# The first 512 tokens of a two-layer SiLU block: five transposes of one contraction tile in place of three, in another order among the weight slabs, and ScalarE's warm-up ahead of the start barrier

## The chip, the core and the metric

The kernel runs on one core of one Trainium2 chip. The metric is the device time of one execution in microseconds (us). Before the change the median of three runs is 124.7 us (124.01 to 125.0). A profile of one further execution gives the time of each instruction and each transfer.

## The reference

Two matrix products with a SiLU between them; inputs and outputs are bfloat16.

```python
B, S, D, F = 1, 2048, 640, 1728
x:  (1, 2048, 640)     w1: (640, 1728)     w2: (1728, 640)

h = jnp.einsum("bsd,df->bsf", x, w1)
h = silu(h)
out = jnp.einsum("bsf,fd->bsd", h, w2)
```

## The kernel before, in words

**Tiles.** The contraction of the first product, D = 640, is cut into five tiles of 128 (`DT`, index k). F = 1728 is cut into 13 tiles of 128 (`FT`, index ft) and a rest of 64. The 2048 tokens are cut into four parts of 512 (`SCH`, index c). The first product needs x with the contraction on the partitions, so every piece of x is brought in by a DMA that transposes it: `turned(c0, c1, k0, k1)` (line 90) brings contraction tiles k0 to k1 of tokens c0 to c1 into `xT`. `w1` comes in slabs: `slab(eng, k, f0, f1)` (line 118) brings tiles f0 to f1 of contraction tile k into `w1s`. Each transfer has a semaphore of its own, and TensorE waits on it where the tile is first read.

**Order of the first product, tokens 0 to 511.** The core has eight accumulation banks (`NO` = 8). For these tokens the loop is turned around: for k = 0 to 4, TensorE sweeps over ft = 0 to 7, one bank each (`sweep`, line 188), so that a sweep needs one slab and one tile of x and not all five. A step is a pair of matmuls, one for each half of 64 output partitions, running beside each other. Sweeps 0 to 2 are in `opening` (line 193); sweep 3 and sweep 4 follow, and after each bank of sweep 4 ScalarE applies SiLU into `hT` (line 175). Slab 0 is cut in two: tiles 0 to 4 (`NA` = 5) come by ScalarE's queue, tiles 5 to 7 by SyncE's (`ld_w1b`), awaited ahead of bank 5. Then come ft = 8 to 12 for the same tokens, from two more loads (`ld_rest`, `ld_rest2`); then tokens 512 on, which wait for all five of their transposes (`ld_xc[c]`, line 159); then the rest of 64, and the second product, whose results are copied out by VectorE and ScalarE and stored.

**What is issued early.** At its start every engine goes through a barrier: it reports that it has arrived and waits for the others. `early(emit, engine, arrived)` (line 98) moves the instructions that `emit` makes ahead of that point of `engine`: with `arrived=False` ahead of the engine's report, so that the barrier opens only after them; with `arrived=True` (only `opening` on TensorE) behind its report, ahead of its wait. All loads for k = 0 to 4 are early on SyncE, one slab is early on ScalarE, and the clearing of `z` is early on VectorE. SyncE issues in the order in which the code stands, and everything after the barrier on this queue (the two rest loads, 15 transposes for the later tokens, `w2`) comes behind the early part.

**The clock and the tables.** Until the first operands have landed, TensorE multiplies zeros (`first_dummies`, line 135): 13 matmuls of 256 columns and one pair of half width. ScalarE applies SiLU to a small cleared tile `warm` (line 153), before which its table load stands; `warm` is cleared by GpSimd at line 140. Both stand behind the barrier.

Of the kernel before, what the change touches and what calls it, by code (L numbers as in the profile page):

```python
# [5 lines left out]
ACT = mybir.ActivationFunctionType  # L6
# [3 lines left out]
def bass_standalone__dense_activation_silu__prompt_kernel(  # L10
# [13 lines left out]
    P = 128  # L24
    NB = 8
    BANK = 512
    DT = D // P
    FT = F // P
    FL = F - FT * P
    SCH = 512  # L30
# [8 lines left out]
    pe, act, dve, pool, sp = nc.tensor, nc.scalar, nc.vector, nc.gpsimd, nc.sync  # L39

    with ExitStack() as es:
        def sb(name, shape, dtype):
            return es.enter_context(nc.sbuf_tensor(name, shape, dtype))
# [9 lines left out]
        warm = sb("warm", [P, 32], fp32)  # L53
# [6 lines left out]
        def sem(name):  # L60
            s = es.enter_context(nc.semaphore(name))
            count[s.name if hasattr(s, "name") else name] = 0
            return [s, 0]

        def tick(ins, s, n=1):
            ins.then_inc(s[0], n)
            s[1] += n
            return (s, s[1])

        def wait(eng, *points):  # L70
            for pt in points:
                if pt is None:
                    continue
                s, v = pt
                key = (id(eng), id(s))
                if seen.get(key, 0) < v:
                    eng.wait_ge(s[0], v)
                    seen[key] = v

        s_pe, s_act, s_dve = sem("s_pe"), sem("s_act"), sem("s_dve")  # L80
        s_pool = sem("s_pool")
# [3 lines left out]
        def load(eng, out_ap, in_ap):  # L85
            s = sem(f"s_ld{n_dma[0]}")
            n_dma[0] += 1
            return tick(eng.dma_start(out=out_ap, in_=in_ap), s, 16)

        def turned(c0, c1, k0, k1):  # L90
            s = sem(f"s_tr{n_dma[0]}")
            n_dma[0] += 1
            return tick(sp.dma_start_transpose(
                out=xT[:, k0:k1, c0:c1], in_=xf[c0:c1, k0 * P:k1 * P]), s, 16)

        ET = mybir.EngineType

        def early(emit, engine, arrived=True):
            n = len(nc.main_func.blocks[0].instructions)
            r = emit()  # L100
            lst = nc.main_func.blocks[0].instructions
            new = lst[n:]
            del lst[n:]
            at = next(
                i for i, ins in enumerate(lst)
                if ins.opcode == ("EventSemaphore" if arrived else "Drain") and ins.engine == engine
            )
            lst[at:at] = new
            return r
# [8 lines left out]
        def slab(eng, k, f0=0, f1=NO):  # L118
            return load(eng, w1s[:, k, f0 * P:f1 * P], w1_v[:, k, f0 * P:f1 * P])

        ld_w1 = {}
        ld_t = {}
        ld_t[0] = ld_t[1] = early(lambda: turned(0, SCH, 0, 2), ET.SP, False)
        ld_w1[0] = early(lambda: slab(act, 0, 0, NA), ET.Activation, False)
        p_z = early(lambda: tick(dve.memset(z[:, :], 0.0), s_dve), ET.DVE, False)  # L125

# [2 lines left out]
        def dummies(n, w):  # L129
            for _ in range(n):  # L130
                for c0 in range(0, P, w):
                    pe.matmul(ps[c0:c0 + w, 3, 0:HB], lhsT=z[:, 0:w], rhs=z[:, :],  # L132
                              start=True, stop=True)

        def first_dummies():
            wait(pe, p_z)
            dummies(13, P)
            dummies(1, HC)

        p_warm = tick(pool.memset(warm[:, :], 0.0), s_pool)  # L140

        ld_w1b = early(lambda: slab(sp, 0, NA, NO), ET.SP, False)
        ld_w1[1] = early(lambda: slab(sp, 1), ET.SP, False)
        ld_w1[2] = early(lambda: slab(sp, 2), ET.SP, False)
        ld_t[2] = early(lambda: turned(0, SCH, 2, 3), ET.SP, False)
        ld_w1[3] = early(lambda: slab(sp, 3), ET.SP, False)
        ld_t[3] = ld_t[4] = early(lambda: turned(0, SCH, 3, DT), ET.SP, False)
        ld_w1[4] = early(lambda: slab(sp, 4), ET.SP, False)
        CM = CO + 2 * P
        ld_rest = load(sp, w1s[:, :, CO:CM], w1_v[:, :, CO:CM])  # L150
        ld_rest2 = load(sp, w1s[:, :, CM:F], w1_v[:, :, CM:F])
        wait(act, p_warm)
        act.activation(out=warm[:, :], in_=warm[:, :], func=ACT.Silu)  # L153

        ld_xc = {}
        for c in range(1, NSC):
            s = sem(f"s_xc{c}")
            for dt in range(DT):
                ld_xc[c] = tick(sp.dma_start_transpose(
                    out=xT[:, dt, c * SCH:(c + 1) * SCH],  # L160
                    in_=xf[c * SCH:(c + 1) * SCH, dt * P:(dt + 1) * P],
# [31 lines left out]
        def opening():  # L193
            first_dummies()
            wait(pe, ld_t[0], ld_w1[0])
            for ft in range(NO):
                if ft == NA:
                    wait(pe, ld_w1b)
                part(0, ft, 0, SCH, start=True)
            for k in (1, 2):  # L200
                sweep(k, 0, SCH, ld_w1[k], ld_t[k])
# [208 lines left out]
```

## Time and profile before

| | before |
|---|---|
| median of three runs | 124.7 us (124.01 to 125.0) |
| profiled execution | 124.91 us |
| its span, first to last instruction | 123.4 us |
| TensorE busy | 121.1 us, 98% of the span |
| ScalarE busy | 38.8 us |
| VectorE busy | 7.0 us |
| HBM read, written | 4.51 MB, 2.62 MB |

The issues on SyncE's queue up to the transposes of tokens 512 to 1023, with the time from the issue's start to the landing:

| what | issued at, us | to landing, us |
|---|---|---|
| x, k = 0 and 1 | 0.00 | 3.7 |
| w1, k = 0, ft 5 to 7 (96 KB) | 1.38 | 3.8 |
| w1, k = 1 (256 KB) | 2.00 | 3.8 |
| w1, k = 2 | 2.53 | 4.0 |
| x, k = 2 | 3.01 | 4.1 |
| w1, k = 3 | 4.20 | 3.7 |
| x, k = 3 and 4 | 4.82 | 4.1 |
| w1, k = 4 | 6.10 | 4.4 |
| w1, ft 8 and 9, all k (320 KB) | 7.09 | 4.3 |
| w1, the rest, all k (560 KB) | 7.53 | 5.5 |
| x, tokens 512 to 1023, five transposes | from 8.10 | the fifth 3.3 |

On ScalarE's queue the first 160 KB of slab 0 are issued at 0.12 and land after 2.7 us.

In the profile, PE is TensorE, PEld its weight loads, ACT ScalarE, DVE VectorE, POOL GpSimd and SP SyncE; a q behind an engine's name marks its issuing part. "L171" is line 171 of the kernel. A row of the timeline has the start, the duration, the engine, line and operation, and, in brackets, how long the engine was idle before and what ended that. The chain of waits is followed back from the last instruction: at each step to whatever released it.

### The profile page before, as it was taken

The numbers are of one execution on the slowest core, as the hardware profiler recorded it, in microseconds if no ns is written. First come the engines' busy times: TensorE is split into PE (matmuls) and PEld (weight loads), VectorE is DVE, ScalarE is ACT, GpSimd is POOL, SyncE is SP. The second block draws the span as 40 slices with busy tenths as digits, with TensorE's granted clock in tenths as the row PEclk, the third lists the DMA queues.
The fourth block names the chain that finished last, engine by engine and source line by source line (L and its number), as shares of the span: only waits on it lengthen the run. The fifth ranks groups of instructions, "written<-read, shape, count | busy, mean of one in ns | idle before, by whom it ended". The sixth has DMA issues, their size and how long they took to land.

```text
span 123.4 us, 2299 instructions
## 1 busy us (share of the span) xinstructions
PE 121.1 (98%) x1057; PEld 59.5 (48%) x1057; DVE 7.0 (6%) x11; ACT 38.8 (31%) x67; POOL 0.3 (0%) x5
## 2 busy tenths in 40 slices
PE   8999999999999999999999999999999999999993
PEld 5455555555555555555544444444444444444452
DVE  0000000000000000000000022002201300222001
ACT  0041985555555555555530011001101200110110
POOL 0000000000000000000000000000000000000000
PEclk9999999999999999999999999999999999999999
DMA  6999945475992000000000005202200220022112
GB/s 142 234 271 302 157 103 108 94 75 92 288 391 70 0 0 0 8 0 0 0 0 5 0 5 115 56 0 106 106 0 5 106 106 0 5 106 106 53 74 86
DMA packets 19482, 10.42 MB, mean 84 GB/s; under 512 B 13457, under 2 KB 18961, under 8 KB 19473
## 3 DMA queue, kind: packets, MB, share of 16 engines
q1 hardware_dynamic: 19184, 10.05, 32.1%
q10 hardware_dynamic: 288, 0.23, 0.8%
q8 instruction: 8, 0.13, 0.5%
q14 instruction: 2, 0.01, 0.0%
HBM read 4.51 MB, written 2.62 MB: 58 GB/s over the span
## 4 chain that ended last, share of the span: by engine, by line
PE 95%; DMA 3%; ACT 0%; issue 0%
PE ps L171 95%; DMA xT<-in_x_dram 3%; ACT o_sb L254 0%
## 5 line engine op out<-in xcount | busy, mean ns | idle before, releaser
L171 PE MATMUL ps<-xT,w1s 128*64 128x512 bf16 x540 | 59.2, 382 | 0.1
L171 PE MATMUL ps<-w2s,hT 64*128 64x512 bf16 (+3 forms) x377 | 46.2, 369 | 0.0
L171 PEld LDWEIGHTS ps<-xT,w1s 128*64 128x64 bf16 x540 | 30.5, 111 | 28.6 <-issue 0.9
L175 ACT ACTIVATE hT<-ps 128x512 bf16<-128x512 f32 x52 | 30.0, 607 | 22.9 <-PE ps L171 22.9
L171 PEld LDWEIGHTS ps<-w2s,hT 64*128 64x128 bf16 (+1 forms) x377 | 21.0, 95 | 24.1 <-issue 0.2
L254 ACT CAST o_sb<-ps 128x512 bf16<-128x512 f32 (+1 forms) x9 | 5.0, 551 | 41.5 <-PE ps L171 41.5
L171 PE MATMUL ps<-hT,w2s 64*128 64x512 bf16 x104 | 11.7, 376 | 0.0
L171 PEld LDWEIGHTS ps<-hT,w2s 64*128 64x128 bf16 x104 | 5.0, 94 | 6.3 <-issue 0.4
L252 DVE CAST o_sb<-ps 128x512 bf16<-128x512 f32 (+1 forms) x8 | 5.4, 675 | 40.5 <-PE ps L171 40.5
L252 DVE CAST oT<-ps 128x512 bf16<-128x512 f32 x2 | 1.4, 692 | 73.8 <-PE ps L171 73.8
L254 ACT CAST oT<-ps 128x512 bf16<-128x512 f32 x2 | 1.2, 586 | 10.6 <-PE ps L171 10.6
L132 PE MATMUL ps<-z 128*128 128x256 bf16 (+1 forms) x15 | 3.3, 419 | 0.4 <-DVE z L125 0.4
L153 ACT ACT_TABLE_LOAD x1 | 1.3, 1283 | 7.1 <-DVEq L395 7.1
L171 PE MATMUL ps<-w2t,hTt 64*128 64x512 bf16 (+2 forms) x17 | 2.9, 363 | 0.0
L132 PEld LDWEIGHTS ps<-z 128*128 128x128 bf16 (+1 forms) x15 | 1.9, 142 | 1.5 <-issue 0.4
L175 ACT ACTIVATE hTt<-ps 128x512 bf16<-128x512 f32 x2 | 1.2, 597 | 1.0 <-PE ps L171 1.0
L171 PEld LDWEIGHTS ps<-w2t,hTt 64*128 64x128 bf16 x17 | 0.9, 94 | 1.1
L171 PE MATMUL ps<-hTt,w2t 64*128 64x512 bf16 x4 | 0.8, 376 | 0.0
L171 PEld LDWEIGHTS ps<-hTt,w2t 64*128 64x128 bf16 x4 | 0.2, 94 | 0.2
L153 ACT ACTIVATE warm<-warm 128x32 f32<-128x32 f32 x1 | 0.2, 229 | 0.0
L125 DVE MEMSET z<- 128x128 uint32 x1 | 0.2, 165 | 0.2 <-issue 0.2
L140 POOL MEMSET warm<- 128x32 f32 x1 | 0.1, 125 | 6.7 <-POOLq L395 6.7
(4 smaller groups left out, 0.4 us busy)
## 6 DMA issues: line engine op xcount, KB each, us to landing
out_dram<-o_sb SPq DMA_DIRECT2D x15, 160.0 KB, 1.8
w2s<-in_w_dram SPq DMA_DIRECT2D x1, 1120.0 KB, 6.1
w1s<-in_w_dram SPq DMA_DIRECT2D x4, 256.0 KB, 3.9
w2s<-in_w_dram SPq DMA_DIRECT2D x1, 960.0 KB, 8.4
w1s<-in_w_dram SPq DMA_DIRECT2D x1, 560.0 KB, 5.5
w1s<-in_w_dram SPq DMA_DIRECT2D x1, 320.0 KB, 4.3
xT<-in_x_dram SPq DMA_TRANSPOSE x18, 3.9
w1s<-in_w_dram ACTq DMA_DIRECT2D x1, 160.0 KB, 2.7
```

The costliest lines, as they stand in the source:

```text
L125: p_z = early(lambda: tick(dve.memset(z[:, :], 0.0), s_dve), ET.DVE, False)
L132: pe.matmul(ps[c0:c0 + w, 3, 0:HB], lhsT=z[:, 0:w], rhs=z[:, :], start=True, stop=True)
L140: p_warm = tick(pool.memset(warm[:, :], 0.0), s_pool)
L153: act.activation(out=warm[:, :], in_=warm[:, :], func=ACT.Silu)
L171: return pe.matmul(o, lhsT=l, rhs=r, start=start, stop=stop, skip_group_check=shared)
L175: r = tick(act.activation(out=out_ap, in_=in_ap, func=ACT.Silu), s_act)
L252: r = tick(dve.tensor_copy(out=out_ap, in_=in_ap), s_dve)
L254: r = tick(act.copy(out=out_ap, in_=in_ap), s_act)
```

## The change

The first 512 tokens' five contraction tiles are brought in by five transposes of one tile each instead of three (tiles 0 and 1, tile 2, tiles 3 and 4). The order on SyncE's queue becomes: x tile 0; rest of slab 0; slab 1; x tiles 1 and 2; slab 2; slab 3; x tiles 3 and 4; slab 4. TensorE multiplies zeros ten times instead of thirteen ahead of the half-width pair. The clearing of `warm` and ScalarE's SiLU on it move ahead of these engines' reports at the barrier. What each sweep waits for is the same by name: slab k and x tile k.

```diff
-        ld_t[0] = ld_t[1] = early(lambda: turned(0, SCH, 0, 2), ET.SP, False)
+        ld_t[0] = early(lambda: turned(0, SCH, 0, 1), ET.SP, False)
         ld_w1[0] = early(lambda: slab(act, 0, 0, NA), ET.Activation, False)
...
         def first_dummies():
             wait(pe, p_z)
-            dummies(13, P)
+            dummies(10, P)
             dummies(1, HC)
 
-        p_warm = tick(pool.memset(warm[:, :], 0.0), s_pool)
+        p_warm = early(lambda: tick(pool.memset(warm[:, :], 0.0), s_pool), ET.Pool, False)
+
+        def warm_up():
+            wait(act, p_warm)
+            act.activation(out=warm[:, :], in_=warm[:, :], func=ACT.Silu)
+
+        early(warm_up, ET.Activation, False)
 
         ld_w1b = early(lambda: slab(sp, 0, NA, NO), ET.SP, False)
         ld_w1[1] = early(lambda: slab(sp, 1), ET.SP, False)
+        ld_t[1] = early(lambda: turned(0, SCH, 1, 2), ET.SP, False)
+        ld_t[2] = early(lambda: turned(0, SCH, 2, 3), ET.SP, False)
         ld_w1[2] = early(lambda: slab(sp, 2), ET.SP, False)
-        ld_t[2] = early(lambda: turned(0, SCH, 2, 3), ET.SP, False)
         ld_w1[3] = early(lambda: slab(sp, 3), ET.SP, False)
-        ld_t[3] = ld_t[4] = early(lambda: turned(0, SCH, 3, DT), ET.SP, False)
+        ld_t[3] = early(lambda: turned(0, SCH, 3, 4), ET.SP, False)
+        ld_t[4] = early(lambda: turned(0, SCH, 4, 5), ET.SP, False)
         ld_w1[4] = early(lambda: slab(sp, 4), ET.SP, False)
         CM = CO + 2 * P
         ld_rest = load(sp, w1s[:, :, CO:CM], w1_v[:, :, CO:CM])
         ld_rest2 = load(sp, w1s[:, :, CM:F], w1_v[:, :, CM:F])
-        wait(act, p_warm)
-        act.activation(out=warm[:, :], in_=warm[:, :], func=ACT.Silu)
```

## The prediction

> **What bounds the kernel now.** I read the chain of waits first. In order of time it is:
>
> ```profile
> 0.00 3.72 DMA xT<-in_x_dram
> 3.72 0.04 issue
> 3.76 117.77 PE ps L171 x1041
> 121.53 0.02 issue
> 121.55 0.27 ACT o_sb L254
> ```
>
> From 3.76 us to 121.53 the chain never leaves TensorE. The total of its idle time before matmuls at line 171 is 0.1 us. So two things alone can move the end: when the real matmuls begin and at what clock, and whether one of them has to wait later on. The change touches only the loads of the first 512 tokens, so the next view is the timeline of the first 18 us (start, duration):
>
> ```profile
> 0.00 1.33 SPq L93 DMA_TRANSPOSE xT<-in_x_dram  x1
> 0.39 3.31 PE L132 MATMUL ps<-z 128*128 128x256 bf16 x15 [0.39 <-DVE z L125]
> 1.38 1.58 SPq L88 DMA_DIRECT2D w1s<-in_w_dram  x3
> 3.01 1.15 SPq L93 DMA_TRANSPOSE xT<-in_x_dram  x1
> ...
> 3.76 0.18 PEld L171 LDWEIGHTS ps<-xT,w1s 128*64 128x64 bf16 x4 [0.36 <-DMA xT<-in_x_dram]
> ...
> 4.20 0.58 SPq L88 DMA_DIRECT2D w1s<-in_w_dram  x1
> 4.82 1.24 SPq L93 DMA_TRANSPOSE xT<-in_x_dram  x1
> 5.42 11.55 PEld L171 LDWEIGHTS ps<-xT,w1s 128*64 128x64 bf16 x108 [0.19 <-issue]
> 6.10 1.95 SPq L88 DMA_DIRECT2D w1s<-in_w_dram  x3
> 8.10 9.81 SPq L159 DMA_TRANSPOSE xT<-in_x_dram  x7
> ```
>
> The reader sees SyncE issuing without a pause, and that a transpose holds it for about the same time whether it carries one contraction tile (1.15) or two (1.33, 1.24). A slab holds it for 0.43 to 0.58. TensorE's pairs of half steps start at 3.76, 4.19, 4.62 and 5.05, 0.43 apart, and from 5.42 on 0.215 apart (54 pairs in 11.55 us). The first pairs run at half rate, though the profile's clock row shows full speed throughout; pair spacing is the better witness.
>
> Sweeps over the eight banks therefore begin at 3.76, 6.28, 8.01, 9.73 and 11.46 and end at 13.19; tiles 8 to 12 end at 18.57, where tokens 512 to 1023 are needed. Against that, the issues' times to landing, asked one by one (start + time to landing): second transpose 3.0 + 4.1 = 7.1, slab 2 at 2.5 + 4.0 = 6.5, slab 3 at 4.2 + 3.7 = 7.9, third transpose 4.8 + 4.1 = 8.9, slab 4 at 6.1 + 4.4 = 10.5, the fifth transpose of the next tokens 13.7 + 3.3 = 17.0. So every operand has just 0.8 to 1.6 us to spare. That slack is the cover that the change spends.
>
> **Part by part: the start.** The first transpose now carries one tile. No row shows such a transpose alone in front of an empty queue; the nearest are these:
>
> ```profile
> L159 SPq DMA_TRANSPOSE xT<-in_x_dram x15: 1261/1262/2413, 8.1 to 28.2; - x15
> DMA to landing us min/median/max: 2.7/3.5/5.5
> ```
>
> It lands between 2.7 (the quickest one-tile transpose) and 3.7 (the double one now). I take 3.0, near the quick end, since nothing is queued before it. Ten dummies and the pair behind them end 3 x 0.215 = 0.64 us sooner, near 2.85, and the first slab from ScalarE lands at 0.12 + 2.7 = 2.8, so neither is later. Real work starts at 3.0, not 3.76. If the clock rises at the same 5.4, that adds about two pairs at half rate: six pairs to 5.5, two at 0.215, and the first sweep ends at 5.95 instead of 6.28. **Gain 0.33 us**; none if the landing stays at 3.7.
>
> [...]
>
> **The issues.** On SyncE the change replaces three transposes by five. First one 1.33 -> about 1.23 (0.09 is what one tile less is worth between 1.24 and 1.15); second 1.15, third 1.15 more, the double one 1.24 -> two of 1.15; 0.05 between issues. The new starts: transpose 0 at 0.00, rest of slab 0 at 1.28, slab 1 at 1.90, transpose 1 at 2.43, transpose 2 at 3.63, slab 2 at 4.82, slab 3 at 5.45, transpose 3 at 5.95, transpose 4 at 7.14, slab 4 at 8.33. Slab 2 moves from 2.53 by **+2.29**, slab 4 from 6.10 by **+2.23**, and with it all behind it on this queue: the two remaining slabs and fifteen transposes of the later tokens.
>
> Time to landing is the unknown. For slabs the ends are 2.7 (the 160 KB slab on ScalarE's empty queue) and 4.4 (slab 4). The nearest row is slab 3, which directly follows a one-tile transpose: 3.7. But that slab landed only 0.8 after the transpose before it, which itself had waited behind two slabs; with issues now further apart less is queued, so I take 3.4. For transposes, ends 2.7 and 4.1; I take 3.3, the row of the fifth one of line 159.
>
> - Sweep 0, bank 5: rest of slab 0 at 1.28 + 3.8 = 5.1; wanted at 3.0 + 5 x 0.43 = 5.15. No stall.
> - Sweep 1, wanted 5.95: slab 1 at 1.9 + 3.8 = 5.7, transpose 1 at 2.43 + 3.3 = 5.75 (6.5 at the far end: stall 0.6). No stall.
> - Sweep 2, wanted 7.68: transpose 2 at 6.9, slab 2 at 4.82 + 3.4 = 8.2 (7.5 to 8.8). **Stall 0.55** (0 to 1.1).
> - Sweep 3, wanted 9.93: slab 3 at 8.9, transpose 3 at 9.3 (10.05). No stall.
> - Sweep 4, wanted 11.66: transpose 4 at 10.4, slab 4 at 8.33 + 3.4 = 11.75 (11.0 to 12.7). **Stall 0.1** (0 to 1.0). The sweep ends at 13.48, 0.3 later than now.
> - The two rest slabs move to 9.32 and 9.77: 9.32 + 4.3 = 13.6 at the loaded time, wanted 13.5; 9.77 + 5.5 = 15.3, wanted 15.6. Nothing taken.
> - Tokens 512 to 1023, wanted 13.48 + 5.38 = 18.86: the fifth transpose is issued at 13.66 + 2.23 = 15.89 and lands at 19.2 (18.6 at 2.7; 20.0 at 4.1). **Stall 0.3** (0 to 1.1).
>
> In that reckoning the early gain and the first stalls don't decide: the shifted queue does. Tokens 1024 to 1535 landed about 9 us before they are wanted (20.6 + 2.8 against 18.57 + 65 x 0.215 = 32.5), and the second weight by 39, while its first use follows the last of the first product at 62.6; 2.23 us more costs nothing there.
>
> **ScalarE's warm-up** now stands before its arrival at the start barrier. Its table load ran from 7.09 for 1.28, its first real work at 11.88; it is hidden now and hidden after. If it stayed behind the barrier, which waits for SyncE, it would run at 9.3 to 10.8, before the first activation near 12. Its slab is issued first, so the load delays nothing. The cleared tile on GpSimd comes earlier by the same move, off every path. Cost 0. PE's wait at the barrier, after sweep 2, ends near 9.3, and sweep 3 starts at 9.9: also covered, but by only 0.6.
>
> **Sum.** Tokens 512 on start at 19.2 in place of 18.57: +0.6. The profiled execution took 124.91 (span 123.4 and 1.5 around it), so 125.5; the median shown is 124.7, 0.2 under it, which gives **125.3**.
>
> **Rivals.**
> 1. *The loaded landings stay* (slower). If time to landing is what one slab costs, not a queue, slab 2 comes at 8.8 and slab 4 at 8.33 + 4.4 = 12.7; sweep 4 ends at 14.46, the next part is wanted at 19.84: +1.3, 126.0. For it: the four 256 KB slabs took 3.7 to 4.4 whatever stood before them. Against: ScalarE's slab took 2.7. It decides from a slab-2 landing of about 8.6 on. Chance 0.22.
> 2. *Issue time is no bound* (faster). The DMA view, cut into 0.05 us slices, shows the double transpose moving at 260 to 310 GB/s near 2.8 us; if slabs land by 2.7 to 3.0 and line 159's first issues shrink from 1.60 to 1.26 with a shorter queue, no stall is left and the start's 0.33 stays: 124.4. Against: SyncE has no idle time up to 29 us. Chance 0.16. [...] The trace disagrees: a 128 KB transpose at such rates moves in under 0.5 us and is issued in 1.15.
> 3. *The clock rises later.* If the first transpose lands at 3.7 and the 0.85 us gap after the dummies starts the count of 5.0 us (0.39 to 5.4) anew, half rate lasts to 8.7: 3.3 us more, worth half, +1.6, 126.3. Chance 0.05.
> 4. *The first landing doesn't come earlier*, as issue time hardly shrinks. The queue's shift still decides, so the time stays 125.3; it is part of the forecast.
>
> **How the numbers follow.** Forecast 125.3 with its own range 124.9 to 125.8, chance 0.57. The whole range takes in rival 2 and most of rival 1, and a clock that rises earlier or later: 124.3 to 126.2. A measurement of this kernel can tell about 1% (1.25 us) from no change. Slower by more: most of rival 1 and rival 3, 0.22. Faster by more: hardly any case, 0.04. Within: 0.74.
>
> **What would show it.** The first pair near 3.0; a new wait of TensorE on slab 2 near 7.7 and one on xT near 18.9; line 159 starting near 10.3; the table load near 0.6. I am wrong if TensorE has no wait after 3.0 (rival 2), if slab 2 takes 3.8 or more to land (rival 1), or if pairs stay 0.43 apart beyond 5.9 (rival 3).

## The result and the profile after

The changed kernel takes 126.34 us (median of six runs, 125.91 to 126.64) against 124.5 for the kernel before (six runs, 124.01 to 125.19): ratio 1.0143, 95% interval 1.0112 to 1.0173, so about 1.8 us slower. The forecast was 125.3 with a range up to 126.2. The profiled execution took 126.50, its span is 125.0. A ratio below can differ by up to 0.2% from the quotient of the two medians, and where the runs of a kernel scatter widely, it leaves the longest out and the range of all runs is given beside it.

The chain of waits of the changed kernel, in order of time (start, duration, what; its last pieces, with the pieces before 15.96 left out):

```profile
15.96 0.04 issue
16.00 4.08 DMA xT<-in_x_dram
20.09 0.04 issue
20.13 91.60 PE ps L177 x846
111.73 0.16 issue
```

Before, the chain entered TensorE at 3.76 and stayed there. Now it runs through SyncE's issues and enters TensorE for good at 20.13, at the first matmul of tokens 512 on, which was at 18.57 before. What released it is the fifth transpose of these tokens, issued at 16.00 and 4.08 us under way. All that follows is as long as before, so 1.56 us of this trace's loss were there by 20.13.

The timeline of the changed kernel (line 177 is what was line 171, line 165 what was line 159):

```profile
0.00 1.25 SPq L93 DMA_TRANSPOSE xT<-in_x_dram  x1
0.53 1.28 ACT L144 ACT_TABLE_LOAD   x1 [0.53 <-issue]
2.38 2.44 SPq L93 DMA_TRANSPOSE xT<-in_x_dram  x2
...
2.99 0.18 PEld L177 LDWEIGHTS ps<-xT,w1s 128*64 128x64 bf16 x4 [0.23 <-DMA xT<-in_x_dram]
...
4.22 0.76 PEld L177 LDWEIGHTS ps<-xT,w1s 128*64 128x64 bf16 x8 [0.19 <-issue]
4.87 1.05 SPq L88 DMA_DIRECT2D w1s<-in_w_dram  x2
5.97 2.42 SPq L93 DMA_TRANSPOSE xT<-in_x_dram  x2
5.97 1.47 PEld L177 LDWEIGHTS ps<-xT,w1s 128*64 128x64 bf16 x16 [0.99 <-issue]
...
7.70 1.47 PEld L177 LDWEIGHTS ps<-xT,w1s 128*64 128x64 bf16 x16 [0.26 <-DMA w1s<-in_w_dram]
8.44 1.95 SPq L88 DMA_DIRECT2D w1s<-in_w_dram  x3
9.59 1.47 PEld L177 LDWEIGHTS ps<-xT,w1s 128*64 128x64 bf16 x16 [0.42 <-issue]
10.44 7.12 SPq L165 DMA_TRANSPOSE xT<-in_x_dram  x5
11.56 3.59 PEld L177 LDWEIGHTS ps<-xT,w1s 128*64 128x64 bf16 x36 [0.51 <-DMA w1s<-in_w_dram]
```

The first real matmul starts at 2.99, and the pairs, 0.43 apart at first, are 0.215 apart from 4.22 on. This close spacing, whose beginning the prediction calls the rise of the clock, began 1.2 us sooner here than in the trace before (5.42). The granted clock reads 1.0 for both profiled executions, so that a clock is behind the spacing is not shown. Yet there is now a start of weight loads with idle time in front at every sweep: 5.97, 7.70, 9.59, 11.56. By the steps between matmuls, TensorE lost 0.7 us ahead of sweep 1 (5.08 to 6.00 in place of 0.215; tile 1 landed at 5.87), nothing ahead of sweep 2, and 0.2 us ahead of each of sweeps 3 and 4. Sweep 4 begins at 11.56, 0.1 later than before in spite of the earlier start and the earlier close spacing. SyncE issues slab 2 at 4.87, slab 4 at 8.44 and line 165's first transpose at 10.44, against 2.53, 6.10 and 8.10.

Further on, the same view for 14 to 22 us:

```profile
15.85 3.43 PE L177 MATMUL ps<-xT,w1s 128*64 128x512 bf16 x30 [0.21 <-DMA w1s<-in_w_dram]
...
20.13 2.13 PE L177 MATMUL ps<-xT,w1s 128*64 128x512 bf16 x18 [0.86 <-DMA xT<-in_x_dram]
```

Two more waits, which the kernel before doesn't have at all: ahead of tile 10, for the second rest load (the step from 15.25 to 15.85 in place of 0.215, so 0.4 us), and ahead of tokens 512 on (the step from 18.87 to 20.13, so 1.0 us). The second is the larger, and what makes the transpose so late is seen in the DMA view of the changed kernel from 15.5 to 19.5 us, in slices of 0.1 us:

```profile
GB/s 187 279 287 289 402 54 249 269 269 271 201 20 0 0 0 0 5 8 10 8 10 10 10 8 13 233 287 297 292 216 197 287 292 287 193 54 79 143 179 187
...
q8 instruction: 1, 0.02, 1.8%
```

From 16.6 to 18.0 nothing but a trickle moves. In front of it, at 15.96 in the list of packets, stands the one packet of the queue for instructions, 16 KB, 1.18 us long. Such packets come again every 10 to 15 us to the end of the run (the next at 26.42, 40.15 and 54.04). They are taken here for TensorE's program code; no view says which engine's instructions they carry, but in two experiments below, with more TensorE instructions, the first one came sooner, at 15.23 and 12.99. The trace before has the same picture two microseconds sooner (packet at 13.80, standstill until 15.75), when these transposes still had 1.6 us to spare; four of the five were through at its end, and here three. The same row of its DMA view from 13.5 to 16.5 us, in slices of 0.075 us:

```profile
GB/s 297 283 287 505 97 161 123 106 184 167 167 116 137 103 85 102 82 45 24 10 27 31 10 10 10 27 10 7 10 14 243 294 294 280 294 270 15 0 0 0
```

### The profile page after: what moved, and what is told of

The parts are those of the page before. It is cut to its first block, busy times and chain, and to the rows that moved or that the text cites. A ratio compares the mean times of both kernels' runs of the same rounds, so it can differ in the third digit from the quotient of the medians.

```text
span 125.0 us, 2296 instructions
## 1 busy us (share of the span) xinstructions
PE 120.9 (97%) x1053; PEld 59.6 (48%) x1054; DVE 6.9 (6%) x11; ACT 38.9 (31%) x67; POOL 0.3 (0%) x5
## 4 chain that ended last, share of the span: by engine, by line
PE 82%; SPq 5%; DMA 3%; issue 0%; ACT 0%
PE ps L177 82%; SPq L165 4%; DMA xT<-in_x_dram 3%; SPq L88 1%; ACT o_sb L260 0%
## 5 line engine op out<-in xcount | busy, mean ns | idle before, releaser
L177 PE MATMUL ps<-xT,w1s 128*64 128x512 bf16 x540 | 59.9, 382 | 1.6 <-DMA xT<-in_x_dram 1.4
L177 PEld LDWEIGHTS ps<-xT,w1s 128*64 128x64 bf16 x540 | 31.1, 111 | 30.2 <-issue 2.1
L132 PE MATMUL ps<-z 128*128 128x256 bf16 (+1 forms) x12 | 2.7, 416 | 0.4 <-DVE z L125 0.4
L132 PEld LDWEIGHTS ps<-z 128*128 128x128 bf16 (+1 forms) x12 | 1.4, 138 | 1.3 <-issue 0.4
```

The costliest lines, as they stand in the source:

```text
L177: return pe.matmul(o, lhsT=l, rhs=r, start=start, stop=stop, skip_group_check=shared)
```

## The experiments

Theory Q: the two added issues push everything behind them on SyncE's queue back by 2.3 us, and that uses up the slack of the later loads. Theory S: the loss lies in the five sweeps, whose operands come late one by one. Ratios are to the kernel before, from the same chip and session.

**The shift alone.** The kernel before, with small loads added behind slab 4:

```diff
         ld_w1[4] = early(lambda: slab(sp, 4), ET.SP, False)
+        junk = sb("junk", [P, 5, 16], bf16)
+        for j in range(5):
+            early(lambda j=j: load(sp, junk[:, j, :], w1_v[:, 0, j * 16:(j + 1) * 16]), ET.SP, False)
```

> The kernel before, unchanged in its transposes, order, dummies and warm-up, with five loads of 4 KB each (into a tile nobody reads) added on SyncE's queue behind slab 4, still ahead of the barrier. They hold SyncE about 5 x 0.48 = 2.4 us, as the change does, but leave the loads of the first 512 tokens alone. Theory Q (what costs is the shift of everything behind the early part of SyncE's queue): line 159's fifth issue moves from 13.7 to 16.1, it lands at 19 to 20 instead of 17, is wanted at 18.6, and the time rises by 0.5 to 1.6 us, ratio 1.004 to 1.013. Theory S (what costs is the later arrival of the single tiles and slabs within the five sweeps): no change, ratio 1.000.

Measured 125.59 against 124.8, ratio 1.0059 (1.0035 to 1.0084). The timeline of TensorE's weight loads in this kernel:

```profile
9.61 8.59 PEld L174 LDWEIGHTS ps<-xT,w1s 128*64 128x64 bf16 x82 [0.62 <-issue]
19.13 1.87 PEld L174 LDWEIGHTS ps<-xT,w1s 128*64 128x64 bf16 x20 [0.94 <-DMA xT<-in_x_dram]
```

The wait ahead of tokens 512 on appears, 0.87 - 0.215 = 0.66 us. A second one, 0.3 us ahead of sweep 3 near 9.4, belongs to none of its operands: slab 3 had landed at 7.7 and the transpose at 8.6. The start barrier, which opens only when SyncE has issued its early part (9.0) and lies ahead of sweep 3, is what is left; here and in the changed kernel sweep 3 starts 0.2 us after SyncE's first issue behind the barrier (9.64 after 9.45, 9.62 after 9.43). So the shift by itself costs about 0.6%: theory Q holds, but it is less than half of the loss.

**The other parts alone.** The kernel before with `dummies(10, P)` and the warm-up moved:

> The kernel before with only the other two parts of the change: ten dummies in place of thirteen, and the warm-up and its clearing ahead of the barrier. The three transposes and the order stay. Theories Q and S alike: within 0.3 us of before, ratio 0.998 to 1.003. Theory C (the gap of 0.85 us between the dummies' end at 2.85 and the first operands at 3.7 delays the clock): up to 1.6 us slower, ratio up to 1.013, and pairs 0.43 apart up to 8 us.

Ratio 1.0017 (0.9977 to 1.0056), but the ten runs reach from 124.33 to 126.65, while the kernel before stays within 124.33 to 125.32. The median of all is 125.55 against 124.8. The profile is of one of the longer runs (126.46), and TensorE's weight loads show what it spent:

```profile
3.72 0.18 PEld L175 LDWEIGHTS ps<-xT,w1s 128*64 128x64 bf16 x4 [0.96 <-DMA xT<-in_x_dram]
...
8.42 1.67 PEld L175 LDWEIGHTS ps<-xT,w1s 128*64 128x64 bf16 x16 [0.25 <-issue]
```

The ten dummies end at 3.06, 0.6 us before the double transpose has landed (3.68), and the pairs stay 0.43 apart until 8.4. What theory C expected happened in this run; that the shortest takes 124.33, as the kernel before does, suggests that it does not happen in every one. In the changed kernel the gap isn't there, since its first transpose lands at 2.95.

**Two loads off SyncE's queue.** In the changed kernel, `ld_rest = load(act, ...)` and `ld_rest2 = load(act, ...)`:

> The changed kernel with the two loads of tiles 8 to 13 (ld_rest, ld_rest2) issued by ScalarE behind the barrier instead of SyncE, which takes about 1.0 us off SyncE's queue ahead of line 165's transposes. Theory Q: the fifth transpose is issued at 15.0 instead of 16.0 and lands about 1 us sooner, near 19.1; time about 125.4, ratio to before 1.005 to 1.010. Theory S: no change against the changed kernel, ratio 1.014.

Ratio 1.0108 (1.0076 to 1.0141), at the edge of what theory Q expected, and its trace isn't what was expected: the fifth transpose was issued at 14.55, 1.45 sooner, and landed at 19.97, practically where it did. With the rest loads on a second queue, these took 5.1 and 6.7 us to land and the transposes beside them 6.5 (median of five), against 3.4, 5.8 and 5.5 in the changed kernel. In this trace tokens 512 on start at 20.01 without a wait of their own: the close spacing began only at 7.0, and TensorE waited 0.2 us for slab 4 and 0.5 us for the first rest load (landed at 14.54). A shorter queue was paid for by slower transfers.

**The fetch of code.** In the changed kernel, three `pe.wait_ge(p_z...)` behind each dummy:

> The changed kernel with 30 waits on an already satisfied semaphore added among TensorE's dummies: same work, more instructions. In the changed kernel's trace one 16 KB transfer on the instruction queue starts at 15.96 and takes 1.18 us, and transpose packets stand still from 16.6 to 18.0; before, it came at 13.8. Theory F (this fetch of TensorE's code, met by the later tokens' transposes, is worth about 1 us of the loss): with more instructions ahead the fetch comes earlier, the fifth transpose lands near 19.0 instead of 20.1, time 125.4, ratio 1.005 to 1.010. If the fetch is only a bystander, or does not move: ratio stays at 1.014.

Ratio 1.0103 (1.0069 to 1.0138). The waits merged into 10 instructions, the packet came at 15.23 instead of 15.96, the standstill went on to 17.1, and the fifth transpose landed at 19.78, with a wait of 1.1 us for it. Not conclusive. A stronger version writes the dummies in smaller pieces:

```diff
-            dummies(10, P)
+            for _ in range(20):
+                for c0 in (0, HC):
+                    pe.matmul(ps[c0:c0 + HC, 3, 0:P], lhsT=z[:, 0:HC], rhs=z[:, 0:P],
+                              start=True, stop=True)
```

> The changed kernel with its ten dummies of 128 x 256 columns written as twenty pairs of half width and 128 columns: about the same time on TensorE, 60 more of its instructions ahead of the real work (30 waits had merged into 10 instructions and moved the code fetch little, so that run didn't decide). Theory F (the fetch of TensorE's code freezes the transposes for about 1.4 us, and costs the changed kernel about 1.2 us because it meets the fifth transpose): the fetch comes 1 to 3 us earlier than 15.96, the fifth transpose, issued near 16.0, lands by 19.0, TensorE's wait for it falls from 1.0 us to under 0.3, and the time to 125.3, ratio 1.003 to 1.008. If the fetch is a bystander: ratio 1.012 to 1.017, as for the changed kernel.

The packet moved to 12.99, the standstill after 16.6 is gone, and the fifth transpose landed 2.9 us after its issue, at 19.37, with no wait for it. But the time didn't follow: ratio 1.0157 (1.0098 to 1.0217), which is what was expected of a bystander. The timeline of TensorE in this kernel:

```profile
12.74 3.19 PE L180 MATMUL ps<-xT,w1s 128*64 128x512 bf16 x28
16.34 6.88 PE L180 MATMUL ps<-xT,w1s 128*64 128x512 bf16 x62 [0.41 <-ACT hT L184]
```

The wait moved to the second rest load, which landed at 16.20, 6.3 us after its issue; that load, not the activation that the view names, is what tile 10 had to wait for. So moving the code packet does move the standstill (transpose packets now stand still until 16.05), but no gain in time shows. In this trace TensorE lost 0.6 us to that load and 0.6 us to slab 2 (landed at 8.35). That the packet delayed the load is not shown, and the trace is of the shortest of four runs (125.94; the others 126.64 to 126.94), so what the others spent isn't seen.

**Three transposes, cut 1/2/2.** The changed kernel with tiles 1 and 2 in one transpose and tiles 3 and 4 in one:

```diff
-        ld_t[1] = early(lambda: turned(0, SCH, 1, 2), ET.SP, False)
-        ld_t[2] = early(lambda: turned(0, SCH, 2, 3), ET.SP, False)
+        ld_t[1] = ld_t[2] = early(lambda: turned(0, SCH, 1, 3), ET.SP, False)
...
-        ld_t[3] = early(lambda: turned(0, SCH, 3, 4), ET.SP, False)
-        ld_t[4] = early(lambda: turned(0, SCH, 4, 5), ET.SP, False)
+        ld_t[3] = ld_t[4] = early(lambda: turned(0, SCH, 3, 5), ET.SP, False)
```

> The changed kernel with tiles 1 and 2 in one transpose and tiles 3 and 4 in one: three transposes as before, cut 1/2/2 and not 2/1/2, the rest of the change kept. SyncE's queue is no longer than before (line 159's transposes start near 8.1). Theory Q with F (shift, and the freeze that then meets the fifth transpose): the wait for tokens 512 on is gone; what is left is the earlier start (0.3 gained) against a wait for tile 1, issued at 2.4 and landing at 6.2: 124.3 to 124.9, ratio 0.996 to 1.002. Theory S (late operands within the sweeps): 125.5 or more, ratio 1.006 and up.

Ratio 1.0030 (1.0001 to 1.0059). With the queue no longer than before, four fifths of the loss are gone. The early start (3.18) still doesn't pay: in the profiled run the close spacing began only at 6.9, and with an early one tile 1, landing at 5.9, is what sweep 1 would wait for (that second half is argued from the landing, since no trace of this kernel has an early close spacing).

**Four transposes**, only tiles 3 and 4 together:

> The changed kernel with tiles 3 and 4 in one transpose: four transposes, SyncE's queue about 1.15 us longer than before instead of 2.3. Theory Q (the shift eats the slack of the loads behind the early part): with no shift the ratio was 1.003, with the whole shift 1.014; half a shift uses up slack more than it costs, so nearer the lower one: 1.004 to 1.008. Theory S (the five single tiles, each late by its own issue): as the changed kernel up to sweep 3, 1.008 to 1.014.

Ratio 1.0090 (1.0057 to 1.0122), between the two, a little above what theory Q expected and inside what theory S did. Three, four and five transposes give 1.003, 1.009 and 1.014: each issue of 1.2 us on SyncE's queue costs about 0.7 us, the shift and the sweeps together.

**Pricing the two late waits.** First the changed kernel without the wait for tokens 512 to 1023, whose first product then reads the first 512 tokens:

```diff
-            wait(pe, ld_xc[c])
+            if c > 1:
+                wait(pe, ld_xc[1], ld_xc[c])
+            x0 = 0 if c == 1 else c * SCH
...
-                    ins = step(b, k, ft, c * SCH, (c + 1) * SCH, start=(k == 0), stop=(k == DT - 1))
+                    ins = step(b, k, ft, x0, x0 + SCH, start=(k == 0), stop=(k == DT - 1))
```

> The changed kernel, but the first product for tokens 512 to 1023 reads the first 512 tokens again and doesn't wait for its own five transposes, which are still issued and are awaited before tokens 1024 on (so the output of these tokens is that of others). All loads as before. Theory Q: the wait of 1.0 us at 19 us in the changed kernel's trace goes and nothing takes its place: 125.3, ratio 1.005 to 1.008. Theory S: the loss lies in the sweeps, and ratio stays above 1.010.

Ratio 1.0078 (1.0052 to 1.0104). Then also without the wait ahead of tile 10 (`wf = ft if ft < NO + 2 else ft - NO` picks the slab, and the load is awaited one part later):

> As the one before, and tiles 10 to 12 of the first 512 tokens read the slabs of tiles 2 to 4 and don't wait for the second rest load either. Theory Q: the wait of 0.6 us ahead of tile 10 goes too; what is left is the waits in the sweeps (1.2 us in the changed kernel's trace, of which the earlier start and clock pay most): 124.4 to 124.9, ratio 0.998 to 1.004. Theory S: ratio 1.008 or more.

Ratio 1.0056 (1.0037 to 1.0076), a little more than expected. The timeline of its weight loads from sweep 4 on is one piece:

```profile
11.56 10.50 PEld L177 LDWEIGHTS ps<-xT,w1s 128*64 128x64 bf16 x100 [0.48 <-DMA w1s<-in_w_dram]
```

Together: 1.0143 - 1.0078 = 0.0065, or 0.8 us, is the wait for the fifth transpose; 0.0022, or 0.3 us, goes with the wait for the second rest load; 0.0056, or 0.7 us, remains (each difference has an uncertainty of 0.3 to 0.4%). The 0.3 us is the least sure. In the profiled run without the wait for tokens 512 on, TensorE waited 0.4 us ahead of tile 8, for the first rest load (landed at 13.64), and not ahead of tile 10:

```profile
13.68 8.61 PE L177 MATMUL ps<-xT,w1s 128*64 128x512 bf16 x78 [0.22 <-DMA w1s<-in_w_dram]
```

Ten of the twelve runs of the kernel with neither wait lie within 125.02 to 125.17. In that kernel's trace the close spacing began at 4.5, and sweep 4 nevertheless started at 11.56, when slab 4 had landed (11.52): the pace of the sweeps is now that of the loads. So theory S has its share; that the 0.7 us lies in the sweeps is read from this trace and has no experiment of its own.

**Thirteen dummies again** in the changed kernel:

> The changed kernel with thirteen dummies again: real work starts at about 3.5 instead of 3.0, since TensorE works through the dummies first. Theory Q: the waits behind swallow it, as they did the gain; 126.2 to 126.5, ratio 1.012 to 1.016. If the early start were worth what was forecast: 0.3 slower still, ratio 1.017.

Ratio 1.0162 (1.0128 to 1.0197). Real work started at 3.49, and the fifth transpose landed at 20.23. Within the intervals this is the changed kernel's time, and the trace shows waits of 0.6 and 1.0 us at the same two places: half a microsecond at the start is worth at most a few tenths here.

**Why the second rest load is late.** The changed kernel without the fifteen transposes of tokens 512 on; the first product of these tokens, and the rest of 64, read the first 512 tokens:

```diff
-            for dt in range(DT):
-                ld_xc[c] = tick(sp.dma_start_transpose(
-                    out=xT[:, dt, c * SCH:(c + 1) * SCH],
-                    in_=xf[c * SCH:(c + 1) * SCH, dt * P:(dt + 1) * P],
-                ), s, 16)
+            ld_xc[c] = None
...
```

> The changed kernel without the fifteen transposes of tokens 512 on; these tokens' first product reads the first 512 tokens instead. Everything ahead on SyncE's queue as in the changed kernel. Theory X (transposes right behind the second rest load in the same rings hold it up): it is issued at 9.9 and lands by 14.0, and no wait is left ahead of tile 10; ratio 1.004 to 1.007, the price of the sweeps alone. Theory L (the load is slow by itself, one DMA engine being late with it): it lands near 15.7 as before, and the wait ahead of tile 10 stays; ratio 1.007 to 1.010.

Ratio 1.0080 (1.0052 to 1.0108), and from the DMA view of its issues from 9 to 14 us:

```profile
w1s<-in_w_dram SPq DMA_DIRECT2D x1, 560.0 KB, 5.6
```

Theory L: the load is late (15.41) without any transpose behind it, with loads of the second weight there instead, though the wait ahead of tile 10 is only 0.15 us in this trace. Its last 896-byte packets thin out: 132 start from 13.5 to 14.0, then 66 and 30 in the next two half microseconds, and the last ends at 15.1. That one DMA engine is late with the load, as theory L has it, is not shown. Why the packets thin out, and why the load takes 4.9 to 6.3 us over the traces with this order of loads and 4.4 from the same issue time in the first experiment, stay open.

**Loads on two queues.** Transposes cut 1/2/2, with the rest of slab 0 and slab 1 issued by ScalarE:

> As the one before (transposes 1/2/2), with the rest of slab 0 and slab 1 issued by ScalarE, ahead of its warm-up: SyncE's queue gets about 1.1 us shorter than before the change, tile 1 and 2 are issued at 1.3. Theory Q with F: first operands at 3.0 to 3.3, no wait in the sweeps, tokens 512 on in time: 0.3 us faster than before, ratio 0.995 to 0.999. A rival R (two queues with transposes and slabs side by side slow each other, as the rest loads on ScalarE's queue did, where the first later transpose took 6.5 us to land): first operands at 3.5 or later and waits in sweeps 1 and 2, ratio 1.002 to 1.010.

Ratio 1.0146 (1.0077 to 1.0215), above what rival R expected. The first transpose landed at 3.61 and not at 3.0, as R had it, but the waits in the sweeps that R named aren't there: the dummies left a gap of 0.6 us, and the close spacing began at 7.4. With only the rest of slab 0 on ScalarE's queue:

> Transposes cut 1/2/2 as in e1_three (ratio 1.003), with only the rest of slab 0 moved to ScalarE's queue, ahead of its warm-up. SyncE's queue gets 0.6 us shorter than before the change, tiles 1 and 2 are issued at 1.8 and land by 5.3. Theory Q (only a longer queue costs): the early start pays at last, ratio 0.996 to 1.000. Rival R (loads from two queues in flight together delay the first transpose, as in e8_two_queues, where it landed at 3.6): first operands later than 3.2, a gap behind the ten dummies, ratio 1.003 to 1.010.

Ratio 1.0125 (1.0088 to 1.0162), again above rival R's range; the first transpose landed at 3.57. Its weight loads, in the longest of the six runs (126.80):

```profile
3.61 0.19 PEld L174 LDWEIGHTS ps<-xT,w1s 128*64 128x64 bf16 x4 [0.85 <-DMA xT<-in_x_dram]
...
9.16 0.81 PEld L174 LDWEIGHTS ps<-xT,w1s 128*64 128x64 bf16 x8 [0.24 <-issue]
```

The operands were there, but the pairs were 0.43 apart until 9.2. And, with the five single transposes again, all of the first weight on ScalarE's queue and only transposes early on SyncE's:

> The changed kernel with every load of the first weight on ScalarE's queue (slabs ahead of its warm-up, the two rest loads behind the barrier) and all transposes alone on SyncE's. SyncE issues the five transposes by 6.0 and the later tokens' from about 6.5. Theory Q: no issue is late any more; first operands at 3.0, no wait, ratio 0.995 to 0.998. Rival R (the two queues slow each other): waits in the sweeps, ratio 1.003 to 1.015.

128.49 against 124.55 (126.36 to 129.61; too scattered for a ratio). The second transpose, issued at 1.31, landed at 9.16, and sweep 1 waited 2.2 us. None of the versions tried is faster than the kernel before.

## Why the prediction was wrong

- **The start** was right: forecast 3.0, measured 2.99. What it is worth was not. The 0.33 us were worked out for a close spacing from 5.4 on, and are swallowed: sweep 1 waited for tile 1 (landed 5.87, wanted 5.3 with the close spacing from 4.22 on), the later sweeps for their slabs.
- **The issues** were right within 0.11 us all along: slab 2 at 4.87 (4.82), slab 4 at 8.44 (8.33), the fifth transpose at 16.00 (15.89).
- **Landing of slabs**: 3.4 taken, 2.8 and 3.1 measured for slabs 2 and 4, against 4.0 and 4.4 before, when the issues stood closer together. The stall of 0.55 us ahead of sweep 2 therefore didn't occur (slab 2 landed at 7.65, the sweep began at 7.73), while sweep 1, reckoned without a stall, lost 0.7 us to tile 1. That speaks against rival 1, whose figure of 126.0 was near but whose mechanism didn't occur: slab 2 landed at 7.65, not 8.6.
- **"The two rest slabs ... Nothing taken"** failed: the second took 5.84 and not 5.5, landed at 15.71 and was wanted at 15.5; the wait is 0.4 us in the trace. The first, due 0.1 after it was wanted by that line's own figures (13.6, 13.5), landed in time at 12.86. Both rest loads are missing from the list that gave "every operand" 0.8 to 1.6 us to spare, and slab 3 in it had 1.8 (landed at 7.9, wanted at 9.73).
- **The step that failed** most is "Tokens 512 to 1023 ... lands at 19.2 ... Stall 0.3". The mechanism was the right one, the shifted queue decides; the term was mis-sized. Time to landing was 4.08, not 3.3. A standstill falls on this transfer here, but it did in the trace before too; what differs is what was left behind it. By the packets, three of the five transposes were through at its end (18.0) and the fifth landed 2.0 us later, against four and 1.1 us before. In five traces with three through (this kernel's, thirteen dummies, the code version with waits, and the two that leave waits out) the fifth took 4.1 to 4.3 us, in the two with four through (the kernel before, four transposes) 3.3 and 3.4; in the shift experiment, with three through, it was issued only as the standstill ended, and took 2.8. Why one more was left was not tried; these transposes had also stood still behind the second rest load, to within 0.5 us of the fifth's issue here and 0.9 before. Tokens 512 on started at 20.13 in place of 19.2, which is nearly the whole of the 1.0 us by which the profiled 126.50 exceeds the 125.5 reckoned for it. The wait is 1.0 us in the trace and worth 0.8 us by the experiment. The far end of 20.0 was written in that very line: it is 1.4 later than 18.57, so 126.1 from this line alone, and the range to 126.2 left next to nothing for the other unknowns.
- **The barrier**, called covered by 0.6, was not: the sweeps were quicker than reckoned, and sweep 3 started at 9.6 with its operands landed at 9.2. About 0.2 us here, 0.3 in the shifted kernel.
- **The baseline.** The trace before is one of its longer runs (124.91; its medians were 124.3 to 124.8). Its slack of 0.8 to 1.6 us holds for a close spacing from 5.42 on. One from 4.22 on, as in the changed kernel, wants every operand about half a microsecond sooner (an estimate: 1.2 us of pairs 0.43 apart in place of 0.215 costs 0.6) and has that much less to spend. I put a clock that rises earlier or later into the range on both sides. No run shows such a clock; what the traces show is the beginning of the close spacing, at 4.22 here, 5.42 before, and 6.9 and 7.0 in two of the experiments (three transposes, and two loads off SyncE's queue). By the reckoning above an early one makes the change dearer.
- **Rival 2** was wrong: issue time is a bound here. Each added issue of 1.2 us on SyncE's queue cost 0.7. **Rival 3** did not occur in this kernel, but the long stretch at 0.43 did in others: in three experiments TensorE was idle for 0.55 to 0.67 us behind the dummies, and the close spacing began at 7.4 (two queues), 8.7 (the other parts alone) and 9.4 (only the rest of slab 0 on ScalarE's queue).
- **ScalarE's warm-up** ran from 0.53 and cost nothing that a trace shows; its share was not measured by itself, only together with the dummies.

## What to carry to other kernels

Splitting a transfer so that its first part lands sooner cost a whole issue of 1.1 to 1.3 us here for every extra part, and everything behind it on that queue paid; so list the slack of each later load on the queue before spending it, down to the last one, and size each landing by its slowest row. A gain at the start is worth something only if the next operands come sooner as well. And take the slack from more than one profile when the pairs' close spacing begins at different times, as it did in the traces here, at 4.2 to 9.4 us: an early one leaves the transfers less time.

## What the runs showed of the hardware

- **Transposes stood still after an instruction packet.** In the kernel before, the first 16 KB packet of the queue for instructions came at 13.80 us with transposes under way: of their 256-byte packets, which take 18 ns in the median, eighteen took 0.36 to 1.30 us and ended together at 15.74 to 15.79. In the changed kernel it came at 15.96, and eighteen took 1.32 to 1.46 us and ended together at 18.01 to 18.05. The second packet, at 24.45 before and 26.42 now, has six beside it of up to 1.43 and 0.98 us, which ended at 26.7 and 28.3. With the first packet at 12.99, in the stronger version of the code experiment, the transposes stood still until 16.05. The instruction packets themselves take 0.9 to 1.4 us in the traces before and after.
- **Transposes stood still beside a slow load, too.** In the kernel before, some transpose packets of over 0.3 us ended together at 12.75 to 12.80, 0.2 us after the last packet of the second rest load (12.56). In the changed kernel they ended at 15.50 to 15.55, after 15.33 and ahead of the instruction packet. Why is not shown, for either case: the traces don't tell which DMA engine a packet ran on.
- **The pairs' spacing.** Where TensorE was idle for about 0.1 us or less between dummies and real work, the pairs reached their close spacing (0.215 in place of 0.43 us) at 4.2 in the changed kernel, 5.4 before and 6.9 with three transposes; with 0.55 to 0.67 us idle, at 7.4, 8.7 and 9.4 in the three experiments named under rival 3. What sets the time is not shown.
- **Two queues.** With one load of 96 KB moved to ScalarE's queue the first transpose landed at 3.57 us, against 2.95 in the changed kernel; with the two rest loads there, the transposes beside them took 6.5 us to land (median of five), against 5.5.
